# A fixed order on every engine, and q and k turned a block at a time, in chunked attention with routed experts

## The chip, the cores and the metric

The kernel runs on one core of a Trainium2 chip. The metric is device microseconds of one launch, from the start of the program to its end. The core has five instruction queues: TensorE (PE; its weight loads are shown apart as PEld), VectorE (DVE), ScalarE (ACT), GpSimd (POOL) and SyncE (SP), which here only issues DMAs. Each queue runs its instructions strictly in the order in which they stand; semaphores make one wait for another.

## The reference

All data is float32. Attention runs on 4 batches x 8 heads x 768 positions x 64, in chunks of 32 queries that see 8 memory keys, the chunk, 16 keys to its left and 8 to its right. Its output, as 3072 tokens x 512, goes to the best of 8 experts each:

```python
for c in range(nc):                                   # nc = 24 chunks
    k_full = np.concatenate([mem_k, k_ctx], axis=2)
    v_full = np.concatenate([mem_v, v_ctx], axis=2)
    scores = scale * np.matmul(q_c, k_full.transpose(0, 1, 3, 2))
    a = np.exp(scores - np.max(scores, axis=-1, keepdims=True))
    a = a / (np.sum(a, axis=-1, keepdims=True) + 1e-09)
    out[:, :, c_start:c_end] = np.matmul(a, v_full)
...
logits = x @ w_gate
expert_idx = np.argmax(logits, axis=1)
...
h = np.maximum(x_sorted[lo:hi] @ w1[e], 0.0)          # per expert e
y_sorted[lo:hi] = h @ w2[e]
return gate_w[:, None] * y
```

## The kernel before, in words

There are two stages. The first is attention in 32 blocks of 96 queries (QB = 96; 8 blocks make a batch), all 8 heads of a block together. The second is the experts: 31 slots of 128 tokens, each with the w1 and w2 (2 MB each) of its expert. The change touches the first stage alone.

A block i goes through these functions, whose tile names are the names in the rows below. `load_v` brings the 128 keys' values of the block (tile v; three DMAs on SP: keys, 8 memory rows, keys). `scores` multiplies the turned keys kT with the turned queries qT into sc (4 matmuls in the code, which the trace shows as 8) and takes three exponentials on ACT into ex. `values` multiplies ex with v into o, heads 0 to 3 and then heads 4 to 7 (16 matmuls in the trace), and DVE divides by the sums (a RECIPROCAL, then a TENSOR_TENSOR into x); POOL then sends x to DRAM. `turn_xb` turns x by four transposes into tx, which DVE or ACT copies to xT. `logits` multiplies xT with the gate matrix into lg_ps (8 matmuls in the trace), which DVE copies to lg. After the eighth block of a batch `route` ranks its tokens: some twenty small DVE instructions, one on ACT, eight additions in a row on POOL (seen), and two small matmuls (rk).

The queries and keys are loaded and turned by halves of a batch, 384 positions at a time (`load_half`: three DMAs of 128 rows for q and three for k; `turn_half`, called three times for a half: four transposes of k into tk, two DVE copies, four transposes of q into tq, two ACT copies to strided columns). The memory keys are turned once (`turn_mem`), and POOL copies them between the keys of each batch. A half serves four blocks; its three turns stand at three of the steps before.

Nothing in the code fixes the order of the queues: the functions are called in a plain loop, and the tile scheduler, which has its own costs and priorities, sets the order on each queue. So the turns of q and k come two or three times in a row, scores run ahead of values, and the work of neighbouring blocks is mixed.

Of the kernel before, what the change touches and what calls it, by code (L numbers as in the profile page):

```python
# [64 lines left out]
HALF = S // 2  # L65
NT = HALF // 128
# [3 lines left out]
NV = 6  # L70


def window(qb):
    return min(max(PER * qb - LEFT, 0), KW - WIN)
# [10 lines left out]
def runs_of(qb):  # L85

    out = []
    for p in range(WIN):
        kind, x = column(window(qb) + p)
        if out and out[-1][1] == kind and out[-1][2] + out[-1][3] == x:  # L90
            out[-1][3] += 1
        else:
            out.append([p, kind, x, 1])
    return out
# [394 lines left out]
def ordinary(ctx, tc, q, k, v, mem_k, mem_v, moe_w_gate, moe_w1, moe_w2, out, good):  # L489
# [16 lines left out]
    lpool = actx.enter_context(tc.tile_pool(name="lpool", bufs=2))  # L506
# [24 lines left out]
    mk = kpool.tile([B * NMEM, H, D], F32, name="mk")  # L531
    for b in range(B):
        nc.scalar.dma_start(mk[NMEM * b : NMEM * b + NMEM], mem_k[b].rearrange("h m d -> m h d"))


    qTs = [kpool.tile([128, H // 2, 2, HALF], F32, name=f"qT{i}") for i in range(2)]
# [19 lines left out]
    half = [dict() for _ in range(2 * B)]  # L556
    turned = {}

    def load_half(m):
        b, hf = divmod(m, 2)  # L560
        for name, src in (("q", q), ("k", k)):
            t = half[m][name] = lpool.tile([128, NT, H, D], F32, name=f"{name}n")
            by = src[b, :, HALF * hf : HALF * hf + HALF].rearrange("h (p t) d -> p t h d", t=NT)
            for j in range(NT):
                nc.sync.dma_start(t[:, j], by[:, j])

    def load_v(i):
        b, qb = divmod(i, NQB)
        st[i]["v"] = vs[i % NV]
        for p, kind, r, n in runs_of(qb):  # L570
            src = (mem_v if kind == "mem" else v)[b, :, r : r + n].rearrange("h r d -> r h d")
            nc.sync.dma_start(st[i]["v"][p : p + n, :, 0:D], src)

    def turn_mem():
        tm = ps_t.tile([128, H // 2, B * NMEM], F32, tag="t", name="tm")
        for a in range(H // 2):
            turn(tm[:, a], mk[:, 2 * a : 2 * a + 2].rearrange("p h d -> p (h d)"), ident[0 : B * NMEM, 0 : B * NMEM])
        turned["mem"] = kpool.tile([128, H // 2, B * NMEM], F32, name="mkT")
        nc.scalar.copy(turned["mem"], tm)

    def turn_half(m, j):

        b, hf = divmod(m, 2)
        if hf == 0 and j == 0:
            turned["k", b] = apool.tile([128, H // 2, KW], F32, name="kT")
            nc.gpsimd.tensor_copy(
                turned["k", b].rearrange("p a (n c) -> p a n c", c=PER)[:, :, :, QB // 2 : QB // 2 + NMEM],
                bc(turned["mem"][:, :, NMEM * b : NMEM * b + NMEM], 2, NQB),
            )
        kT = turned["k", b].rearrange("p a (n c) -> p a n c", c=PER)  # L590
        qT = turned["q", m] = qTs[m % 2]
        tk = ps_t.tile([128, H // 2, 128], F32, tag="t", name="tk")
        for a in range(H // 2):
            turn(tk[:, a], half[m]["k"][:, j, 2 * a : 2 * a + 2].rearrange("p h d -> p (h d)"), ident)  # L594
        by = tk.rearrange("p a (n f c) -> p a n f c", n=NQB // 2, f=2)
        for f in range(2):
            c0 = (QB // 2 + NMEM) * f + j
            nc.vector.tensor_copy(  # L598
                kT[:, :, hf * NQB // 2 : (hf + 1) * NQB // 2, c0 : c0 + QB // 2 - NT + 1 : NT], by[:, :, :, f]
            )  # L600
        tq = ps_t.tile([128, H // 2, 128], F32, tag="t", name="tq")
        for a in range(H // 2):
            turn(tq[:, a], half[m]["q"][:, j, 2 * a : 2 * a + 2].rearrange("p h d -> p (h d)"), ident)  # L603
        for x in range(2):
            sl = slice(D * x, D * x + D)
            nc.scalar.copy(qT[sl, :, x, j : j + HALF - NT + 1 : NT], tq[sl])  # L606

    def scores(i):
        s, (b, qb) = st[i], divmod(i, NQB)
        kT, qT = turned["k", b], turned["q", i // (NQB // 2)]  # L610
        q0 = QB * (qb % (NQB // 2))
        w0 = window(qb)
        sc = ps_s.tile([128, 2, 512], F32, tag="s", name="sc")
        for a in range(H // 2):
            o = sc[:, a // 2, 2 * QB * (a % 2) : 2 * QB * (a % 2) + 2 * QB]
            mm(  # L616
                o.rearrange("p (x t) -> p x t", x=2),
                lhsT=kT[:, a, w0 : w0 + WIN],
                rhs=qT[:, a, :, q0 : q0 + QB],
                start=True,  # L620
                stop=True,
            )
        ex = s["ex"] = apool.tile([128, H, QB], F32, name="ex", bufs=3)
        x = 0 if qb == 0 else 2 if qb == NQB - 1 else 1
        sc4 = sc[:, :, 0 : 4 * QB].rearrange("p g (h t) -> p g h t", h=4)
        ex4 = ex.rearrange("p (g h) t -> p g h t", g=2)
        for g in range(3):
            sl = slice(CHUNK * g, CHUNK * g + CHUNK)
            nc.scalar.activation(  # L629
                ex4[:, :, :, sl], sc4[:, :, :, sl], AF.Exp, bias=mask[:, 3 * x + g : 3 * x + g + 1], scale=D**-0.5  # L630
            )

    def values(i):
        s = st[i]
        s["x"] = apool.tile([QB, H, D], F32, name="x", bufs=3)
        for g in range(2):
            o = ps_o.tile([QB, 4, D + 1], F32, tag="o", name="o")
            for j in range(4):
                h = 4 * g + j
                mm(o[:, j], lhsT=s["ex"][:, h], rhs=s["v"][:, h], start=True, stop=True)  # L640

            inv = inv_all[:, i, 4 * g : 4 * g + 4]
            nc.vector.reciprocal(inv, o[:, :, D])
            nc.vector.tensor_tensor(s["x"][:, 4 * g : 4 * g + 4], o[:, :, 0:D], bc(inv, 2, D), op=OP.mult)  # L644
        s["x"] = s["x"].rearrange("p h d -> p (h d)")
        nc.gpsimd.dma_start(x_dram[QB * i : QB * i + QB], s["x"])  # L646

    def turn_xb(i):
        s = st[i]
        tx = ps_t.tile([128, DM // 128, QB], F32, tag="t", name="tx")  # L650
        for c in range(DM // 128):
            turn(tx[:, c], s["x"][:, 128 * c : 128 * c + 128], ident[0:QB, 0:QB])  # L652
        s["xT"] = apool.tile([128, DM // 128, QB], F32, name="xT")
        (nc.vector.tensor_copy, nc.scalar.copy)[i % 2](s["xT"], tx)
# [3 lines left out]
    def logits(i):  # L658
        s, (b, t) = st[i], divmod(i, NQB)
        if t == 0:  # L660
            lgs[b] = rpool.tile([QB, NQB, E], F32, name="lg")
        ps = ps_t.tile([QB, E], F32, tag="t", name="lg_ps")
        for c in range(DM // 128):
            mm(ps, lhsT=s["xT"][:, c], rhs=wg[:, c], start=c == 0, stop=c == DM // 128 - 1)  # L664
        nc.vector.tensor_copy(lgs[b][:, t], ps)
        if t == NQB - 1:
            route(b)


    def small(shape, name, dt=F32):  # L670
        return rpool.tile(shape, dt, name=name)

    def route(b):
# [12 lines left out]
        nc.vector.tensor_tensor(oh, bc(rev[0:QB], 1, NQB), bc(first, 2, E), op=OP.is_equal)  # L686

        nc.vector.tensor_tensor(l, l, bc(top, 2, E), op=OP.subtract)
        nc.scalar.activation(l, l, AF.Exp)
        total = small([QB, NQB], "total")  # L690
        nc.vector.reduce_sum(total, l, axis=AX_X)
        nc.vector.tensor_scalar(total, total, 1e-9, None, op0=OP.add)
        nc.vector.reciprocal(gate[:, sl], total)

# [4 lines left out]
        mm(rk, lhsT=ones[0:QB, 0:QB], rhs=seen[:, sl], start=False, stop=True)  # L699
        own = small([QB, NQB, E], "own")  # L700
        nc.vector.tensor_tensor(own, rk, oh, op=OP.mult)
        rank = small([QB, NQB], "rank")
        nc.vector.reduce_sum(rank, own, axis=AX_X)
        ri = small([QB, 3, NQB], "ri", I32)
# [5 lines left out]
        nc.vector.tensor_copy(low, ri[:, 1])  # L710
        for t in range(NQB):
            nc.vector.tensor_scalar(
                row_of[:, t0 + t], iota[0:QB], low[:, t : t + 1], None, op0=OP.is_equal
            )


    load_half(0)
    load_v(0)
    load_v(1)
    load_half(1)  # L720
    turn_mem()
    for j in range(NT):
        turn_half(0, j)
    for i in range(NB + 3):
        m = i // (NQB // 2)
        if i % (NQB // 2) == 1 and m + 2 < 2 * B:
            load_half(m + 2)
        if i + 2 < NB:
            load_v(i + 2)
        if i < NB:  # L730
            scores(i)
        if i % (NQB // 2) < NT and m + 1 < 2 * B:
            turn_half(m + 1, i % (NQB // 2))
        if 0 <= i - 3 < NB:
            logits(i - 3)
        if 0 <= i - 1 < NB:
            values(i - 1)
        if 0 <= i - 2 < NB:
            turn_xb(i - 2)
# [174 lines left out]
```

## Time and profile before

| | |
|---|---|
| three runs | 720.2, 721.64 and 726.11 us; median 721.64 |
| the profiled execution | 721.35 us; its span from first to last instruction 719.6 us |
| the page's share of busy time | PE 90%, PEld 71%, DVE 19%, ACT 18%, POOL 13% |
| mean granted clock of TensorE | 0.927 of 2.4 GHz |
| bytes moved by DMA | 172.78 MB, 240 GB/s over the span |

The profile is of one execution. The span is what lies between the first and the last instruction, so 1.75 us of the time lie outside it. The share of PE is a mean over two stages with different limits, and a matmul that runs at the lower of the two clocks (1.2 in place of 2.4 GHz) counts as busy for about twice as long, so the share alone does not tell how much of the time could be had back. Matmuls overlap, so the distance from the start of one group to the start of the next, where nothing waits, is what a group costs; the length in a row is longer by the tail of its last matmul.

### The profile page before, as it was taken

To read this page: it belongs to the slowest core of one execution; us is meant where nothing else is said; L and a number is where in the kernel's file an instruction comes from. 1 tells how busy PE (TensorE), PEld (TensorE's weight loads), DVE (VectorE), ACT (ScalarE), POOL (GpSimd) and SP (SyncE) were. 2 spreads that over 40 slices of the span, in tenths; PEclk is the share of its full clock that TensorE was granted. 3 is DMA by queue.
4 is the path that set the end of the run, shared out by engine and by line. 5 is a ranking of instruction groups with operands and counts; after the bars stand their busy time and mean duration, and the time that the engine had idled before them with its cause. 6 is when DMAs were issued, how large, how long until landed. Compare 5 with 4: busy or idle time off the path is not lost. (4 is left out here: it accounts for less than half of the span.)

```text
span 719.6 us, 9964 instructions
## 1 busy us (share of the span) xinstructions
PE 648.2 (90%) x4036; PEld 510.3 (71%) x4036; DVE 137.6 (19%) x406; ACT 127.0 (18%) x228; POOL 92.1 (13%) x144
## 2 busy tenths in 40 slices
PE   2888898898883699999999999999999999999991
PEld 2887787788772677776777677767776777677760
DVE  3334534435425010010001000100010001000100
ACT  3554435345200001100110011001100110011000
POOL 2001101101102111111111111111111111111000
PEclk9999969969955579999999999999999999999996
DMA  9999837723212948998899989998899889998800
GB/s 182 206 171 179 173 68 153 166 53 77 73 34 92 392 155 302 321 337 325 313 322 334 342 302 319 333 338 323 314 336 328 325 308 332 328 328 297 319 3 3
DMA packets 140520, 172.78 MB, mean 240 GB/s; under 512 B 87662, under 2 KB 87790, under 8 KB 140464
## 3 DMA queue, kind: packets, MB, share of 16 engines
q1 hardware_dynamic: 132496, 151.01, 66.9%
q0 software_dynamic: 7008, 20.72, 8.4%
q8 instruction: 34, 0.56, 0.3%
q10 hardware_dynamic: 960, 0.32, 0.2%
q14 instruction: 22, 0.18, 0.1%
HBM read 159.44 MB, written 14.42 MB: 242 GB/s over the span
## 5 line engine op out<-in xcount | busy, mean ns | idle before, releaser
L835 PEld LDWEIGHTS ph<-xsT,w 128*128 128x128 f32 x1984 | 228.4, 193 | 14.6 <-issue 14.4
L835 PE MATMUL ph<-xsT,w 128*128 128x128 f32 x1984 | 228.7, 277 | 0.0
L852 PE MATMUL py<-w,h 128*128 128x512 f32 x496 | 218.0, 592 | 0.0
L852 PEld LDWEIGHTS py<-w,h 128*128 128x128 f32 x496 | 91.9, 190 | 103.7 <-issue 103.7
L844 DVE TENSOR_SCALAR h<-ph 128x512 f32<-128x512 f32 x31 | 21.5, 692 | 403.7 <-issue 381.7
L854 ACT ACTIVATE y<-py,gates 128x512 f32<-128x512 f32 x31 | 21.3, 687 | 317.9 <-PE py L852 308.1
L616 PE MATMUL sc<-qT,kT 128*128 128x192 f32 x256 | 58.3, 354 | 9.2 <-ACT ex L629 4.2
L855 POOL DMA_INDIRECT out_dram<-y,dst x31 | 31.5, 1016 | 242.5 <-ACT y L854 242.5
L640 PE MATMUL o<-v,ex 128*96 128x65 f32 x512 | 58.5, 276 | 1.4 <-ACT ex L629 1.4
L640 PEld LDWEIGHTS o<-v,ex 128*96 128x96 f32 x512 | 57.0, 193 | 1.9 <-ACT ex L629 1.9
L812 POOL DMA_INDIRECT xs<-x_dram,src x31 | 30.2, 974 | 170.0 <-PE txs L823 154.6
L616 PEld LDWEIGHTS sc<-qT,kT 128*128 128x128 f32 x256 | 42.3, 199 | 13.0 <-ACT ex L629 6.1
L629 ACT ACTIVATE ex<-sc,cst 128x256 f32<-128x256 f32 x96 | 38.5, 471 | 70.8 <-PE o L640 63.2
L606 ACT COPY qT<-tq 64x512 f32<-64x512 f32 x48 | 40.0, 834 | 31.8 <-PE tq L603 29.8
L846 ACT ACTIVATE h<-ph 128x512 f32<-128x512 f32 x31 | 18.5, 597 | 126.6 <-PE ph L835 126.6
L664 PEld LDWEIGHTS lg_ps<-wg,xT 128*96 128x96 f32 x256 | 29.7, 192 | 13.5 <-PE tq L603 7.3
L664 PE MATMUL lg_ps<-wg,xT 128*96 128x8 f32 x256 | 30.5, 246 | 8.8 <-DVE kT L598 5.2
L646 POOL DMA_DIRECT2D x_dram<-x x32 | 16.6, 520 | 163.6 <-DVE x L644 159.0
L652 PE MATMUL tx<-cst,x 96*128 96x96 f32 x128 | 24.2, 287 | 4.9 <-DVE x L644 2.8
L644 DVE TENSOR_TENSOR x<-o,inv_all 96x256 f32<-96x256 f32 x64 | 26.9, 420 | 2.1
L823 PE MATMUL txs<-cst,xs 128*128 128x128 f32 x124 | 19.4, 283 | 6.9 <-DMA xs<-x_dram,src 6.9
L598 DVE COPY kT<-tk 128x256 f32<-128x256 f32 x48 | 20.5, 487 | 26.6 <-PE tk L594 23.9
(76 smaller groups left out, 225.9 us busy)
## 6 DMA issues: line engine op xcount, KB each, us to landing
w<-in_moe_w_dram SPq DMA_DIRECT2D x62, 2048.0 KB
qn<-in_q_dram SPq DMA_DIRECT2D x24, 256.0 KB
kn<-in_k_dram SPq DMA_DIRECT2D x24, 256.0 KB
x_dram<-x POOLq DMA_DIRECT2D x32, 192.0 KB, 3.0
v<-in_v_dram SPq DMA_DIRECT2D x24, 128.0 KB
v<-in_v_dram SPq DMA_DIRECT2D x24, 112.0 KB
v<-in_v_dram SPq DMA_DIRECT2D x8, 144.0 KB
v<-in_v_dram SPq DMA_DIRECT2D x8, 96.0 KB
```

The lines of the kernel that those rows point to most:

```text
L606: nc.scalar.copy(qT[sl, :, x, j : j + HALF - NT + 1 : NT], tq[sl])
L616: mm(o.rearrange("p (x t) -> p x t", x=2), lhsT=kT[:, a, w0 : w0 + WIN], rhs=qT[:, a, :, q0 : q0 + QB], start=True, stop=True,)
L629: nc.scalar.activation(ex4[:, :, :, sl], sc4[:, :, :, sl], AF.Exp, bias=mask[:, 3 * x + g : 3 * x + g + 1], scale=D**-0.5)
L640: mm(o[:, j], lhsT=s["ex"][:, h], rhs=s["v"][:, h], start=True, stop=True)
L644: nc.vector.tensor_tensor(s["x"][:, 4 * g : 4 * g + 4], o[:, :, 0:D], bc(inv, 2, D), op=OP.mult)
L652: turn(tx[:, c], s["x"][:, 128 * c : 128 * c + 128], ident[0:QB, 0:QB])
L664: mm(ps, lhsT=s["xT"][:, c], rhs=wg[:, c], start=c == 0, stop=c == DM // 128 - 1)
L812: nc.gpsimd.indirect_dma_start(out=s["x"], out_offset=None, in_=x_dram, in_offset=bass.IndirectOffsetOnAxis(ap=src[:, a : a + 1], axis=0),)
L835: mm(ph[:, f], lhsT=s["w1"][:, c, c0 : c0 + 128], rhs=s["xT"][:, c], start=c == 0, stop=c == DM // 128 - 1,)
L844: nc.vector.tensor_scalar(o, ph, 0.0, None, op0=OP.max)
L852: mm(py, lhsT=s["h"][:, f], rhs=s["w2"][:, f], start=f == 0, stop=f == F // 128 - 1)
L855: nc.gpsimd.indirect_dma_start(out=out, out_offset=bass.IndirectOffsetOnAxis(ap=dst[:, a : a + 1], axis=0), in_=y, in_offset=None, bounds_ ...
```

## The change

The first stage is written inside `tc.manual_schedule()`: every queue now runs its instructions in the order in which the code calls them. q and k are loaded and turned a block at a time: `load_q` is one DMA of 96 rows, `load_k` brings the block's 96 keys with the 8 memory keys already between them (three DMAs of 48, 8 and 48 rows), and `turn_q` and `turn_k` are four transposes each, with two ACT copies and one DVE copy. `load_half`, `turn_mem` and POOL's copies of the memory keys go. The loads have four buffers in place of two and are called two to four blocks ahead, ex has two buffers in place of three, and there are four qT tiles of a block in place of two of a half. `values` is called by halves with `turn_xb` of the block before between them. The logits are written to the unused end of the PSUM bank that holds the second half of o; ACT alone copies xT. `route` becomes a generator that the loop advances by one piece in each step.

```diff
+    def load_k(i):
+        st[i]["kn"] = lpool.tile([PER, H, D], F32, name="kn")
+        load_runs(st[i]["kn"], i, PER * (i % NQB), PER, k, mem_k)
...
+    def turn_k(i):
         b, qb = divmod(i, NQB)
...
+            turn(tk[:, a], st[i]["kn"][:, 2 * a : 2 * a + 2].rearrange("p h d -> p (h d)"), ident[0:PER, 0:PER])
+        nc.vector.tensor_copy(turned[b][:, :, PER * qb : PER * qb + PER], tk)
...
+        bank = ps_o.tile([QB, 512], F32, tag="o", name="o")
+        o = bank[:, 0 : 4 * (D + 1)].rearrange("p (h d) -> p h d", h=4)
...
+        return bank[:, 4 * (D + 1) :]
...
-        ps = ps_t.tile([QB, E], F32, tag="t", name="lg_ps")
+        ps = room[:, 0:E]
...
         for t in range(t0, t0 + NQB):
             nc.gpsimd.tensor_tensor(seen[:, t + 1], seen[:, t], onehot[:, t], op=OP.add)
         rk = ps_t.tile([QB, NQB, E], F32, tag="t", name="rk")
         mm(rk, lhsT=tri[0:QB, 0:QB], rhs=oh, start=True, stop=False)
         mm(rk, lhsT=ones[0:QB, 0:QB], rhs=seen[:, sl], start=False, stop=True)
+        yield 1
...
+    def routing(room=None):
+        if work and next(work[0], None) is None:
+            work.pop(0)
+
+    with tc.manual_schedule():
...
+        for i in range(NB + 3):
+            need(i + 4, load_k)
+            need(i + 3, load_q)
+            need(i + 2, load_v)
+            need(i + 2, turn_q)
+            need(i, scores)
+            if 0 <= i - 1 < NB:
+                values(i - 1, 0)
+            need(i - 2, turn_xb)
+            if 0 <= i - 1 < NB:
+                room = values(i - 1, 1)
+            else:
+                room = ps_o.tile([QB, 512], F32, tag="o", name="o")
+            need(i + 3, turn_k)
+            if 0 <= i - 3 < NB:
+                logits(i - 3, room)
+                if (i - 3) % NQB == NQB - 1:
+                    work.append(route((i - 3) // NQB))
+            routing()
+        while work:
+            routing()
```

**On PE in a step of the loop.** Before, around the end of a batch, this stands in a row (tk and tq are the turns of k and q, lg_ps the logits, sc the scores, o the values, tx the turns of x):

```order
L616 MATMUL sc<-qT_101,kT 128x192 x4
L640 MATMUL o<-v_110,ex 96x65 x8
L616 MATMUL sc<-qT_101,kT 128x192 x4
L594 MATMUL tk<-cst,kn 128x128 x4
L603 MATMUL tq<-cst,qn 128x128 x4
L664 MATMUL lg_ps<-wg,xT 96x8 x4
L652 MATMUL tx<-cst,x 128x96 x4
L594 MATMUL tk<-cst,kn 128x128 x4
L603 MATMUL tq<-cst,qn 128x128 x4
L664 MATMUL lg_ps<-wg,xT 96x8 x4
L640 MATMUL o<-v_111,ex 96x65 x8
```

Two sets of turns and logits stand between one scores and the next values. Now every step reads like this one, of block 12 (its scores read qT_95), with the values of block 11 (v_112):

```order
L574 MATMUL tq<-cst,qn 128x96 x4
L593 MATMUL sc<-qT_95,kT 128x192 x4
L619 MATMUL o<-v_112,ex 96x65 x4
L633 MATMUL tx<-cst,x 128x96 x4
L619 MATMUL o<-v_112,ex 96x65 x4
L584 MATMUL tk<-cst,kn 128x104 x4
L645 MATMUL o<-wg,xT 96x8 x4
```

Scores and values come once in every step. The logits stand last and write into the bank of the second o; between that o and them stand only the four turns of k.

**On PE and POOL where a batch is ranked.** At the end of the step of block 13 the two rk matmuls stand in PE's queue, ahead of the next step's turns and scores:

```order
L619 MATMUL o<-v_107,ex 96x65 x4
L584 MATMUL tk<-cst,kn 128x104 x4
L645 MATMUL o<-wg,xT 96x8 x4
L680 MATMUL rk<-onehot,cst 96x64
L681 MATMUL rk<-seen,ones 96x64
L574 MATMUL tq<-cst,qn 128x96 x4
```

On POOL the additions that the second rk waits for (seen) stand behind the stores of x of blocks 0 to 12, the last of which waits for the values of the same step:

```order
L541 MEMSET seen 96x8
L626 DMA x_dram<-x 96x512 x13
L678 ISA
L678 TENSOR_TENSOR seen<-seen,onehot 96x8 x8
L626 DMA x_dram<-x 96x512 x9
```

The rk of the next two batches stand in the same way in the steps of blocks 22 and 31 (nine stores further each), and the last one after the loop. Before, the two rk and the additions had other work between them.

**On SP.** Before, the loads of v for a block, then those of a half, then v again:

```order
L572 DMA v_106<-in_v_dram 56x8x64
L565 DMA qn<-in_q_dram 128x8x64 x3
L565 DMA kn<-in_k_dram 128x8x64 x3
L572 DMA v_107<-in_v_dram 64x8x64
L572 DMA v_107<-in_mem_v_dram 8x8x64
L572 DMA v_107<-in_v_dram 56x8x64
```

Now a step of the loop:

```order
L555 DMA kn<-in_k_dram 48x8x64
L555 DMA kn<-in_mem_k_dram 8x8x64
L555 DMA kn<-in_k_dram 48x8x64
L560 DMA qn<-in_q_dram 96x8x64
L555 DMA v_110<-in_v_dram 64x8x64
L555 DMA v_110<-in_mem_v_dram 8x8x64
L555 DMA v_110<-in_v_dram 56x8x64
```

A step issues seven DMAs, where before it issued three, and six larger ones for every four blocks.

## Rows read from the trace of the kernel before

**Rows 1.** Windows by stage: start:end, length, busy of each engine, clock, DMA, GB/s

```profile
0.00:18.70 18.70, 5.34 (x28) 4.08 (x29) 5.41 (x9) 6.53 (x8) 3.96 (x15) 1.00 1.12 183
18.70:219.40 200.70, 175.80 (x1332) 158.89 (x1332) 83.00 (x293) 80.39 (x157) 22.15 (x58) 0.87 0.60 122
219.40:252.90 33.50, 15.76 (x72) 15.39 (x73) 9.09 (x43) 0.26 (x1) 7.27 (x12) 0.50 0.71 266
252.90:719.60 466.70, 451.29 (x2604) 331.95 (x2604) 40.14 (x62) 39.80 (x62) 58.70 (x59) 0.98 0.82 291
```

**Rows 2.** Windows inside the attention stage, same columns

```profile
54.00:92.00 38.00, 32.45 (x273) 29.04 (x272) 18.52 (x68) 15.38 (x31) 5.47 (x16) 0.99 0.86 169
92.00:105.50 13.50, 13.02 (x71) 12.06 (x70) 3.80 (x13) 6.20 (x11) 1.02 (x2) 0.50 0.21 48
...
143.00:157.00 14.00, 13.38 (x73) 12.59 (x73) 4.58 (x15) 6.21 (x11) 1.02 (x2) 0.51 0.18 41
...
197.70:219.40 21.70, 17.61 (x97) 15.19 (x96) 6.99 (x23) 2.16 (x5) 2.05 (x4) 0.50 0.13 37
```

**Rows 3.** Timeline of PE at the full clock: start, length, operation, count

```profile
28.83 0.60 PE L594 MATMUL tk<-cst,kn 128*128 128x128 f32 x4
...
29.70 1.16 PE L640 MATMUL o<-v,ex 128*96 128x65 f32 x12
30.69 0.50 PE L652 MATMUL tx<-cst,x 96*128 96x96 f32 x4
31.03 1.49 PE L616 MATMUL sc<-qT,kT 128*128 128x192 f32 x8
32.36 0.77 PE L664 MATMUL lg_ps<-wg,xT 128*96 128x8 f32 x8
32.98 1.55 PE L640 MATMUL o<-v,ex 128*96 128x65 f32 x16
```

**Rows 4.** Timeline of PE where the clock falls

```profile
89.25 0.81 PE L664 MATMUL lg_ps<-wg,xT 128*96 128x8 f32 x8 [0.66 <-DVE kT L598]
...
91.52 0.78 PE L603 MATMUL tq<-cst,qn 128*128 128x128 f32 x4 [0.21 <-DVE xT L654]
...
93.64 2.80 PE L640 MATMUL o<-v,ex 128*96 128x65 f32 x16
```

**Rows 5.** Timeline of all engines, last blocks and the ranking after them

```profile
187.33 1.50 PE L640 MATMUL o<-v,ex 128*96 128x65 f32 x16
...
189.07 0.42 DVE L644 TENSOR_TENSOR x<-o,inv_all 96x256 f32<-96x256 f32 x1
189.55 0.20 PEld L652 LDWEIGHTS tx<-cst,x 96*128 96x128 f32 x2 [0.42 <-DVE x L644]
...
189.79 0.51 POOL L646 DMA_DIRECT2D x_dram<-x  x1 [4.45 <-DVE x L644]
...
219.28 0.16 DVE L665 COPY lg<-lg_ps 96x8 f32<-96x8 f32 x1 [1.64 <-PE lg_ps L664]
...
220.87 2.12 POOL L696 TENSOR_TENSOR seen<-seen,onehot 96x8 f32<-96x8 f32 x8 [3.53 <-DVE total L691]
...
224.69 1.65 DVE L712 TENSOR_SCALAR row_of<-cst,low 96x128 f32<-96x128 f32 x8
```

**Rows 6.** Timeline of all engines, the start; SPq rows are DMA issues

```profile
3.26 4.26 SPq L565 DMA_DIRECT2D kn<-in_k_dram  x3
...
10.09 1.11 PE L594 MATMUL tk<-cst,kn 128*128 128x128 f32 x4
...
14.34 0.60 PE L594 MATMUL tk<-cst,kn 128*128 128x128 f32 x4
...
24.33 3.89 SPq L565 DMA_DIRECT2D kn<-in_k_dram  x3
...
33.25 0.54 SPq L572 DMA_DIRECT2D v<-in_mem_v_dram  x1
...
34.93 0.52 SPq L572 DMA_DIRECT2D v<-in_mem_v_dram  x1
```

More of the change, by code (lines that the diff above doesn't have):

```diff
@@ L61, in _consts_general @@
     return np.ascontiguousarray(pack), at
-HALF = S // 2
-NT = HALF // 128
 WIN = 128
@@ L69 @@
 KW = NQB * PER
-NV = 6
+NV, NQ = 6, 4
 def window(qb):
@@ L82, in column, with runs @@
     return "key", QB * blk + (r if r < QB // 2 else r - NMEM)
-def runs_of(qb):
+def runs(start, n):
     out = []
-    for p in range(WIN):
-        kind, x = column(window(qb) + p)
+    for p in range(n):
+        kind, x = column(start + p)
         if out and out[-1][1] == kind and out[-1][2] + out[-1][3] == x:
@@ L505, in ordinary @@
     kpool = actx.enter_context(tc.tile_pool(name="kpool", bufs=1))
-    lpool = actx.enter_context(tc.tile_pool(name="lpool", bufs=2))
+    lpool = actx.enter_context(tc.tile_pool(name="lpool", bufs=4))
     apool = actx.enter_context(tc.tile_pool(name="apool", bufs=2))
@@ L529, in ordinary @@
     nc.scalar.dma_start(wg, moe_w_gate.rearrange("(c p) e -> p c e", p=128))
[L531 to L536, printed above, removed]
+    qTs = [kpool.tile([128, H // 2, 2, QB], F32, name=f"qT{i}") for i in range(NQ)]
     for i, t in enumerate(qTs):
@@ L555, in ordinary @@
     st = [dict() for _ in range(NB)]
-    half = [dict() for _ in range(2 * B)]
     turned = {}
[L559 to L565, printed above, removed]
-    def load_v(i):
-        b, qb = divmod(i, NQB)
[L569 to L572, printed above, removed]
@@ L574, in turn_mem @@
-    def turn_mem():
-        tm = ps_t.tile([128, H // 2, B * NMEM], F32, tag="t", name="tm")
-        for a in range(H // 2):
[L577 to L606, printed above, removed]
@@ new lines, in load_runs, with load_q @@
+    def load_runs(to, i, start, n, src, mem):
+        for p, kind, r, n in runs(start, n):
+            ap = (mem if kind == "mem" else src)[i // NQB, :, r : r + n].rearrange("h r d -> r h d")
+            nc.sync.dma_start(to[p : p + n], ap)
+    def load_q(i):
+        b, qb = divmod(i, NQB)
+        t = st[i]["qn"] = lpool.tile([QB, H, D], F32, name="qn")
+        nc.sync.dma_start(t, q[b, :, QB * qb : QB * qb + QB].rearrange("h r d -> r h d"))
+    def load_k(i):
+        st[i]["kn"] = lpool.tile([PER, H, D], F32, name="kn")
+        load_runs(st[i]["kn"], i, PER * (i % NQB), PER, k, mem_k)
@@ new lines, in load_v, with turn_q @@
+    def load_v(i):
+        st[i]["v"] = vs[i % NV]
+        load_runs(st[i]["v"][:, :, 0:D], i, window(i % NQB), WIN, v, mem_v)
+    def turn_q(i):
+        qT = st[i]["qT"] = qTs[i % NQ]
+        tq = ps_t.tile([128, H // 2, QB], F32, tag="t", name="tq")
+        for a in range(H // 2):
+            turn(tq[:, a], st[i]["qn"][:, 2 * a : 2 * a + 2].rearrange("p h d -> p (h d)"), ident[0:QB, 0:QB])
+        for x in range(2):
+            nc.scalar.copy(qT[D * x : D * x + D, :, x], tq[D * x : D * x + D])
@@ L608, in scores @@
+    def turn_k(i):
+        b, qb = divmod(i, NQB)
+        if qb == 0:
+            turned[b] = apool.tile([128, H // 2, KW], F32, name="kT")
+        tk = ps_t.tile([128, H // 2, PER], F32, tag="t", name="tk")
+        for a in range(H // 2):
+            turn(tk[:, a], st[i]["kn"][:, 2 * a : 2 * a + 2].rearrange("p h d -> p (h d)"), ident[0:PER, 0:PER])
+        nc.vector.tensor_copy(turned[b][:, :, PER * qb : PER * qb + PER], tk)
     def scores(i):
         s, (b, qb) = st[i], divmod(i, NQB)
-        kT, qT = turned["k", b], turned["q", i // (NQB // 2)]
@@ L611, in scores @@
-        q0 = QB * (qb % (NQB // 2))
         w0 = window(qb)
@@ L617, in scores @@
                 o.rearrange("p (x t) -> p x t", x=2),
-                lhsT=kT[:, a, w0 : w0 + WIN],
-                rhs=qT[:, a, :, q0 : q0 + QB],
+                lhsT=turned[b][:, a, w0 : w0 + WIN],
+                rhs=s["qT"][:, a],
                 start=True,
@@ L622, in scores @@
             )
-        ex = s["ex"] = apool.tile([128, H, QB], F32, name="ex", bufs=3)
+        ex = s["ex"] = apool.tile([128, H, QB], F32, name="ex")
         x = 0 if qb == 0 else 2 if qb == NQB - 1 else 1
@@ L631, in scores, with values @@
             )
-    def values(i):
+    def values(i, g):
         s = st[i]
[L635 to L646, printed above, removed]
+        if g == 0:
+            s["x"] = apool.tile([QB, H, D], F32, name="x", bufs=3)
+        bank = ps_o.tile([QB, 512], F32, tag="o", name="o")
+        o = bank[:, 0 : 4 * (D + 1)].rearrange("p (h d) -> p h d", h=4)
+        for j in range(4):
+            h = 4 * g + j
+            mm(o[:, j], lhsT=s["ex"][:, h], rhs=s["v"][:, h], start=True, stop=True)
+        inv = inv_all[:, i, 4 * g : 4 * g + 4]
+        nc.vector.reciprocal(inv, o[:, :, D])
+        nc.vector.tensor_tensor(s["x"][:, 4 * g : 4 * g + 4], o[:, :, 0:D], bc(inv, 2, D), op=OP.mult)
+        if g == 1:
+            s["x"] = s["x"].rearrange("p h d -> p (h d)")
+            nc.gpsimd.dma_start(x_dram[QB * i : QB * i + QB], s["x"])
+        return bank[:, 4 * (D + 1) :]
     def turn_xb(i):
@@ L653, in turn_xb, with logits @@
         s["xT"] = apool.tile([128, DM // 128, QB], F32, name="xT")
-        (nc.vector.tensor_copy, nc.scalar.copy)[i % 2](s["xT"], tx)
+        nc.scalar.copy(s["xT"], tx)
     lgs = {}
-    def logits(i):
+    def logits(i, room):
         s, (b, t) = st[i], divmod(i, NQB)
@@ L665, in logits @@
         nc.vector.tensor_copy(lgs[b][:, t], ps)
-        if t == NQB - 1:
-            route(b)
     def small(shape, name, dt=F32):
@@ L686, in route @@
         nc.vector.tensor_tensor(oh, bc(rev[0:QB], 1, NQB), bc(first, 2, E), op=OP.is_equal)
+        yield 1
         nc.vector.tensor_tensor(l, l, bc(top, 2, E), op=OP.subtract)
         nc.scalar.activation(l, l, AF.Exp)
+        yield 1
         total = small([QB, NQB], "total")
@@ L693, in route @@
         nc.vector.reciprocal(gate[:, sl], total)
+        yield 1
         for t in range(t0, t0 + NQB):
@@ L699, in route @@
         mm(rk, lhsT=ones[0:QB, 0:QB], rhs=seen[:, sl], start=False, stop=True)
+        yield 1
         own = small([QB, NQB, E], "own")
@@ L703, in route @@
         nc.vector.reduce_sum(rank, own, axis=AX_X)
+        yield 1
         ri = small([QB, 3, NQB], "ri", I32)
@@ L710, in route @@
         nc.vector.tensor_copy(low, ri[:, 1])
+        yield 1
         for t in range(NQB):
@@ L714, in route, with need @@
             )
[L717 to L739, printed above, removed]
+            if t % 3 == 2:
+                yield 1
+    def need(i, f, *lists):
+        if 0 <= i < NB:
+            f(i)
+    work = []
+    def routing(room=None):
+        if work and next(work[0], None) is None:
+            work.pop(0)
+    with tc.manual_schedule():
+        for i in range(3):
+            load_k(i)
+            load_q(i)
+            if i < 2:
+                load_v(i)
+        load_k(3)
+        turn_k(0)
+        turn_q(0)
+        turn_k(1)
+        turn_q(1)
+        turn_k(2)
+        for i in range(NB + 3):
[19 more added lines that the diff above has]
+            routing()
     ok = cpool.tile([QB, 2, NB, H], F32, name="ok")
```

## The prediction

> **What bounds the kernel now.** I read the stages first. Up to 18.7 us the core waits for its first loads, from there to 219.4 us it runs the attention blocks, from there to 252.9 us it ranks the tokens and loads the first experts, and the rest, 466.7 us, is expert work with PE busy in 451 of it [rows 1]. The change touches the first two stretches. The last two start from the last logits copy at 219.28 us and have the same instructions as before, so I move them as one block.
>
> Inside the 200.7 us of attention, PE is busy for 175.8, yet DVE and ACT for only about 83 and 80 and DMA for 0.60 [rows 1]. So PE's order decides. Windows over that stretch split it in two kinds [rows 2]. At a granted clock of 0.99 PE still idles 5.6 of 38 us. At 0.50 it is busy nearly all the time, and slow: 13.5, 14.0 and 21.7 us, together 49.2. At the full clock the same work would take about half, so some 24 us lie here. Before the first of these falls PE had run logits, turns and little else for about four microseconds, with waits between; afterwards sixteen value matmuls take 2.80 us, which take 1.55 elsewhere [rows 3, 4]. In the third stretch, 197.7 to 219.4, there are no scores left to run, and each block's chain of values, division, turn and logits stands bare.
>
> **What a block needs.** From start to start where nothing waits [rows 3]: eight turns of 128 columns take 29.70 - 28.83 = 0.87 us, 0.109 each; twelve value matmuls 0.99, so sixteen 1.32; four turns of x 0.34; eight scores 1.33; eight logits 0.62. Before, a block has on average six turns of q and k (24 for four blocks), 0.65 us: 4.26 in all, 136 us for 32 blocks. Of 200.7 us, then, 136 is work at the full clock, some 24 the low clock and some 40 idle time.
>
> **The change, part by part.** The new turns are eight a block, but narrower: four of 96 columns at the price of x's turns, 0.34, and four of 104, 0.36. A block's work becomes 4.31 us, 0.05 more. ACT's copies of q become contiguous, DVE's copy of k one in place of parts, POOL's copies of the memory keys go; all of this lies beside PE, since DVE and ACT have about 2.6 and 2.5 us of work a block now [rows 1].
>
> The order adds a wait in each step. The logits write the bank that DVE is still reading for the second half of x. In the trace the end of a values group to the first turn that needs its x is 187.33 + 1.50 to 189.55, 0.72 us; PE could have started 0.17 earlier than that end, as a turn does at 30.69 against 29.70 + 1.16 [rows 3, 5]. That makes 0.89, of which the four turns of k fill 0.36: 0.53 us left. Behind the logits on PE stand the next turns of q and all scores, so the wait is on the path. The step becomes 4.84 us. Each step also has new waits for DMA on PE (k, q, v); the trace shows none for such steps. They cost nothing if already satisfied, and at most about what PE idles today, 5.6 us in 38, that is 0.9 a block of 6.2, less the 0.53 already counted: 0 to 0.4. I take 0.15, nearer the low end, because PE's idle rows name engines and not such checks. **Step: 5.0 us.**
>
> SP must feed this. Three loads of 1,024 short rows take 3.89 us to issue, 1.30 each, and a block's v (three DMAs, as many rows) 34.93 - 33.25 = 1.68 [rows 6]. A step now wants 0.81 of such a load for k with one small DMA more (0.5), 0.75 for q, and v: 1.05 + 0.5 + 0.98 + 1.68 = 4.2 us. That is under 5.0, and the buffers let SP run some three blocks ahead, so PE hides it; if that cover went, the step would be what DMA gives.
>
> Start: ahead of the first scores stand k, q and two v of blocks 0 to 2, 1.71 MB, and 0.25 MB of constants. At the 183 GB/s of the first stretch that is 10.7 us after the first bytes [rows 1]; in the trace the first k is issued at 3.26 and turned at 10.09 [rows 6], so a load is several microseconds on its way. I take the first scores at 14 us, bounds 12 and 18.7 (as now). The next three steps have little PE work and go as loads come, 4 us each: block 3 starts at 26. From there 28 steps of 5.0 bring the scores of block 31 to 166.
>
> Ranking: in the steps of blocks 13, 22 and 31 PE meets the second rk matmul while POOL still has to store the same step's x (0.51) and do eight additions (2.12) [rows 5]. These start when DVE's division ends, as the logits do. So PE waits 2.63 - 0.62 - 0.1 = 1.9 us. Two of these lie ahead of the last scores, 3.8 us. They also leave PE with turns, logits and idle time for some 4 us, like the stretch in rows 4. I expect the clock to fall in each, and to come back with the next scores: half of a 7 us stretch, 3.4 us each, bounds 0 and 6.7 (half of the 13.5 of rows 2). Scores of block 31 then start at 166 + 3.8 + 6.8 = 176.6.
>
> Tail: block 31's step without new turns and with the third rk, 4.31 - 0.70 + 0.53 + 1.9 = 6.0; the next 0.34 + 1.32 + 0.62 + 0.53 = 2.8; turn, copy and logits of the last block 2.2. That is 11.0 us at the full clock. Scores are gone here as they were after 197.7, so I add 5 for the low clock (bounds 0 and 9). The last logits copy ends at about 192.6. One batch's ranking is still unfinished there, and its eight row_of instructions, 1.65 us [rows 5], now stand ahead of the last ranking: 194.3. Before, that copy ended at 219.44.
>
> **Sum:** 194.3 - 219.44 = -25.1 us. Against the profiled execution's 721.35 that is 696.2; the median of the three runs, 721.64, is the same within 0.3, so **I forecast 696 us**.
>
> **A rule against it.** Between 10.09 and 14.34 us PE ran only turns, and four of them went from 1.11 to 0.60 us: turning alone brought the clock from 1.2 to 2.4 GHz [rows 6]. The Trainium skill says otherwise (TensorE: Matmul & The Clock Gate, Part 4): transposes do not count as work that raises the clock. By that rule the 1.0 us of turns in each new step would be as good as idle time, and the third rival below would be the likely one. The trace disagrees with it here.
>
> **The rivals.** First, *no falls*: the clock holds through the rk waits and the tail and the step is 4.84. That takes off 6.8 + 5 + 28 x 0.16 = 16 us: 680. For it: from 54 to 92 us the clock held through many half-microsecond waits. Against it: no row shows it holding through 4 us without scores.
>
> Second, *the loads bound the step*. In the busiest loading DMA's share was already 0.86 with only 6.2 us a block [rows 2], a step of 5.0 wants as many bytes, and seven DMAs share the queue. If SP and DMA give 5.6 us a step, the time is 696 + 28 x 0.6 = 713. It would show as PE waiting for DMA ahead of turns. Against it stands the sum of 4.2.
>
> Third, on the slow side, *the clock does not hold in the ordinary step*. Each step now has 3.5 us from the end of its scores to the next scores, with values as the only large work between. If that lets the clock fall, work of 4.31 doubles while the wait of 0.53 vanishes: 3.8 us more per such step. The forecast's 25 us are gone after 25 / 3.8 = 6.6 such steps beyond the two counted; with ten, the time is 734. For it: before the fall of rows 4 PE was not idle, only poor in scores and values. Against it: there neither scores nor values ran at all, here 2.65 of 5 us are theirs, more than the 2.65 of 6.3 that held from 54 to 92.
>
> That the order is not what the code says is no rival; the built order shows it.
>
> **How the numbers follow.** The forecast's case gets 0.66, no falls 0.13, loads 0.12, the clock 0.05, and 0.04 is left for what I have not thought of. The forecast's own bounds: with steps of 4.9, one fall less and a short tail about 686; with steps of 5.2 and full falls about 708. The range takes in the first rival and the second to its larger side: 678 to 715. About 1%, 7 us, is what a measurement of this kernel can tell from no change. Faster by over 1% (under 714) then holds 0.66 + 0.13 + half of the loads' case and some of the rest, 0.86; same 0.08; slower 0.06.
>
> **What would show it.** Right: PE's row reads the same in every step, 4.8 to 5.2 us from scores to scores; logits wait for DVE some 0.5 us in most steps; rk waits for POOL about 1.9 us three times; low clock only there, at the start and in the tail; the last logits copy near 193, and everything after it as long as before. Wrong: PE waits for loads in the middle of the stage, a low clock in ordinary steps, or a change behind the last logits.

## The result, and the profile after

| | before | this |
|---|---|---|
| median of the device times | 723.76 us (720.2 to 726.11, 4 runs) | 693.11 us (689.9 to 695.51, 4 runs) |
| ratio, 95% interval | | 0.9578 [0.9514, 0.9642] |
| profiled execution | 721.35 us | 695.51 us, span 693.7 |

The change makes the kernel 30.7 us, 4.2%, faster; the forecast was 696 us, 25.1 us less. That forecast was made from the profiled execution, and between the two profiled executions lie 25.8 us. The profiled execution of this kernel is the slowest of its four (granted clock 0.946; the others 0.951 to 0.955), so by the medians the gain is 5.6 us larger than forecast. Of the other executions there is no trace, so where these 5.6 us lie is open. Line numbers of the new kernel differ: scores L593, values L619, division L622 and L623, turns of x L633, of q L574, of k L584, ranking L678 to L697. The logits, L645, appear as "o", since they stand in the bank of the values.

First the windows by stage of the kernel after, then windows inside its attention, with the columns of [rows 1]: start:end, length, busy time (and instructions) of PE, PEld, DVE, ACT, POOL, the granted clock, DMA's share, GB/s.

```profile
0.00:16.00 16.00, 5.09 (x25) 3.86 (x25) 3.45 (x8) 3.17 (x5) 2.02 (x15) 1.00 1.09 152
16.00:192.60 176.60, 156.72 (x1398) 149.95 (x1396) 69.76 (x256) 79.52 (x191) 21.39 (x56) 0.93 0.75 146
192.60:229.70 37.10, 17.68 (x80) 16.82 (x81) 11.64 (x52) 0.26 (x1) 7.80 (x13) 0.50 0.66 248
229.70:693.70 464.00, 448.91 (x2598) 329.95 (x2596) 39.45 (x61) 39.81 (x62) 58.17 (x59) 0.99 0.81 293
...
55.00:75.00 20.00, 18.55 (x181) 17.75 (x181) 8.80 (x31) 10.07 (x24) 2.05 (x4) 1.00 1.08 202
...
86.30:89.70 3.40, 3.23 (x13) 3.23 (x14) 0.00 (x0) 0.94 (x2) 0.32 (x2) 0.50 0.98 166
134.10:140.90 6.80, 6.39 (x32) 6.35 (x33) 0.60 (x2) 2.63 (x6) 0.48 (x3) 0.50 0.41 82
181.80:192.60 10.80, 8.47 (x52) 8.05 (x51) 3.48 (x18) 0.96 (x2) 1.88 (x8) 0.50 0.12 36
```

Against [rows 1] the gain is all in attention: from the first scores to the last logits 176.6 us instead of 200.7, and the start is 2.7 shorter. What follows the last logits copy has hardly changed: 501.1 us of span remain after it starts, 500.3 before. Against [rows 2] the low clock inside attention is down from 49.2 us to 21 (3.4, 6.8 and 10.8), and a fourth stretch of some 3 us lies in the start, from 24.97.

PE's timeline of the kernel after, as in [rows 3, 4]: start in us, length, operation, and in brackets the idle time before it and what ended it. The first rows are the start, then comes one ordinary step, then the step of block 13 with the first ranking.

```profile
5.33 0.93 PE L584 MATMUL tk<-cst,kn 104*128 104x104 f32 x4 [5.33 <-DMA kn<-in_k_dram]
...
15.95 2.51 PE L593 MATMUL sc<-qT,kT 128*128 128x192 f32 x8
...
24.97 0.87 PE L574 MATMUL tq<-cst,qn 96*128 96x96 f32 x4 [1.71 <-DMA qn<-in_q_dram]
...
30.59 1.49 PE L593 MATMUL sc<-qT,kT 128*128 128x192 f32 x8
...
55.21 1.49 PE L593 MATMUL sc<-qT,kT 128*128 128x192 f32 x8
56.54 0.81 PE L619 MATMUL o<-v,ex 128*96 128x65 f32 x8
57.19 0.50 PE L633 MATMUL tx<-cst,x 96*128 96x96 f32 x4
57.53 0.82 PE L619 MATMUL o<-v,ex 128*96 128x65 f32 x8
58.18 0.53 PE L584 MATMUL tk<-cst,kn 104*128 104x104 f32 x4
59.07 0.84 PE L645 MATMUL o<-wg,xT 128*96 128x8 f32 x8 [0.36 <-DVE x L623]
59.77 0.53 PE L574 MATMUL tq<-cst,qn 96*128 96x96 f32 x4
60.14 1.49 PE L593 MATMUL sc<-qT,kT 128*128 128x192 f32 x8
...
83.71 0.84 PE L645 MATMUL o<-wg,xT 128*96 128x8 f32 x8 [0.37 <-DVE x L623]
84.41 0.36 PE L680 MATMUL rk<-onehot,cst 96*96 96x64 f32 x2
86.47 0.58 PE L681 MATMUL rk<-seen,ones 96*96 96x64 f32 x2 [1.71 <-POOL seen L678]
86.85 0.85 PE L574 MATMUL tq<-cst,qn 96*128 96x96 f32 x4
87.49 2.58 PE L593 MATMUL sc<-qT,kT 128*128 128x192 f32 x8
```

From 55.21 to 60.14 is one step, 4.93 us, and nearly all read alike: the hand-made order with its one idle time, ahead of the logits. In the last rows the second rk matmul waits 1.71 us for POOL's additions, and the eight scores after it take 2.58 us where they took 1.49: the clock has fallen. The chain of events in the end part, timeline of all engines, answers to [rows 5]:

```profile
181.58 2.13 POOL L678 TENSOR_TENSOR seen<-seen,onehot 96x8 f32<-96x8 f32 x8
...
192.58 0.16 DVE L646 COPY lg<-o 96x8 f32<-96x8 f32 x1 [0.49 <-PE o L645]
192.66 1.65 DVE L697 TENSOR_SCALAR row_of<-cst,low 96x128 f32<-96x128 f32 x8
```

The eight row_of instructions end at 194.31. And the waits of the same kernel up to 230 us, summed by what was waited for (total, times, longest):

```profile
PEld o L645 <- DVE x L623: 16.1, 28, 0.9
...
PE tk L584 <- DMA kn<-in_k_dram: 10.3, 3, 5.3
...
PE rk L681 <- POOL seen L678: 5.9, 4, 1.7
...
PE tq L574 <- DMA qn<-in_q_dram: 2.3, 2, 1.7
```

PE waits for the loads in the start only: the three waits of tk end at 5.33, 9.33 and 14.37, and the two of tq at 10.83 and 24.97. In the steps two things remain, the logits' wait for the division and rk's for POOL.

### The profile page after: what moved, and what is told of

It is laid out like the page before. It is cut to its first block, busy times and chain, and to the rows that moved or that the text cites. A ratio compares the mean times of both kernels' runs of the same rounds, so it can differ in the third digit from the quotient of the medians.

```text
span 693.7 us, 10193 instructions
## 1 busy us (share of the span) xinstructions
PE 628.4 (91%) x4096; PEld 500.6 (72%) x4096; DVE 124.3 (18%) x376; ACT 122.8 (18%) x259; POOL 89.4 (13%) x142
## 5 line engine op out<-in xcount | busy, mean ns | idle before, releaser
L619 PE MATMUL o<-v,ex 128*96 128x65 f32 x512 | 54.4, 251 | 0.0
L619 PEld LDWEIGHTS o<-v,ex 128*96 128x96 f32 x512 | 53.4, 172 | 0.1
L593 PE MATMUL sc<-qT,kT 128*128 128x192 f32 x256 | 52.6, 353 | 0.0
L593 PEld LDWEIGHTS sc<-qT,kT 128*128 128x128 f32 x256 | 45.5, 208 | 0.0
L576 ACT COPY qT<-tq 64x384 f32<-64x384 f32 x64 | 30.2, 472 | 69.1 <-PE tq L574 68.7
L645 PE MATMUL o<-wg,xT 128*96 128x8 f32 x256 | 28.5, 238 | 12.3 <-DVE x L623 12.2
L645 PEld LDWEIGHTS o<-wg,xT 128*96 128x96 f32 x256 | 25.9, 175 | 18.0 <-DVE x L623 16.1
L584 PE MATMUL tk<-cst,kn 104*128 104x104 f32 x128 | 18.1, 267 | 10.4 <-DMA kn<-in_k_dram 10.3
L623 DVE TENSOR_TENSOR x<-o,inv_all 96x256 f32<-96x256 f32 x64 | 26.9, 420 | 2.2
L622 DVE RECIPROCAL inv_all<-o 96x4 f32<-96x4 f32 x64 | 11.4, 179 | 84.1 <-PE o L619 84.0
```

Of the source, the lines that this page charges most:

```text
L576: nc.scalar.copy(qT[D * x : D * x + D, :, x], tq[D * x : D * x + D])
L593: mm(o.rearrange("p (x t) -> p x t", x=2), lhsT=turned[b][:, a, w0 : w0 + WIN], rhs=s["qT"][:, a], start=True, stop=True,)
```

## Experiments

Diffs are against the kernel after where nothing else is said; each ratio is to the kernel before, timed beside it. "Steps" are the distances from scores to scores.

**1. The logits' wait.** The logits' eight columns go into the spare part of the bank of the first half of o, which DVE has read by then.

```
-                values(i - 1, 0)
+                room = values(i - 1, 0)
...
-                room = values(i - 1, 1)
+                values(i - 1, 1)
```

> The logits go to the bank of the first half of o, which DVE has read long before, so their wait for DVE (16.1 us over 28 steps in the changed kernel's trace) is gone. If that wait is on the path as the prediction says, a step falls from 4.93 to about 4.4 us and the time from 693 to about 678. If the loads are the next bound, steps come out at 4.6 to 4.8, PE shows waits for DMA, and the time is 683 to 689. If the wait only hid another wait of the same length, nothing changes.

Measured: 677.67 us (676.71 to 680.44), ratio 0.9361 [0.9301, 0.9421]. Ordinary steps took 4.32 us, the sum of a block's PE work (4.31). PE's timeline of this kernel:

```profile
59.60 0.53 PE L584 MATMUL tk<-cst,kn 104*128 104x104 f32 x4
59.96 0.77 PE L645 MATMUL o<-wg,xT 128*96 128x8 f32 x8
60.59 0.53 PE L574 MATMUL tq<-cst,qn 96*128 96x96 f32 x4
```

The logits now follow the turns of k without idle time. So the choice of a bank cost 0.60 us a step and some 15 us in all, half of what the whole change brought, and the loads carry steps of 4.32 as well. Both rk waits stayed (2.3 and 2.2 us), and their low clock too.

**2. The ranking's wait.** Two pieces of the ranking go into one step and rk gets a step of its own: POOL's additions come a step earlier, rk stays in the step in which it stood.

```
         nc.vector.tensor_tensor(oh, ...)
-        yield 1
...
             nc.gpsimd.tensor_tensor(seen[:, t + 1], ...)
+        yield 1
         rk = ps_t.tile([QB, NQB, E], F32, tag="t", name="rk")
```

> The eight additions on POOL run one step ahead of the matmul that reads them; the number of pieces of the ranking stays the same. If the waits of rk and the two falls of the clock behind them belong together, as the prediction says, the steps of blocks 13, 14, 22 and 23 (7.65, 6.01, 7.55 and 7.51 us) fall to about 4.93 and the third wait goes from the tail: 9 + 1.8, so about 682. If the clock falls there for another reason, only the waits go, 5.5 us, and the falls stay: about 688.

Measured: 684.81 us (680.0 to 685.62), ratio 0.9432 [0.9365, 0.9498]. From the scores of block 3 to those of block 31 it takes 138.0 us instead of 146.3. PE's timeline at the first ranking, at the last logits and scores ahead of the end part, and a window of this kernel:

```profile
83.02 0.36 PE L680 MATMUL rk<-onehot,cst 96*96 96x64 f32 x2
83.22 0.33 PE L681 MATMUL rk<-seen,ones 96*96 96x64 f32 x2
...
161.80 0.84 PE L645 MATMUL o<-wg,xT 128*96 128x8 f32 x8 [0.72 <-DVE x L623]
...
166.51 0.81 PE L645 MATMUL o<-wg,xT 128*96 128x8 f32 x8 [0.82 <-DVE x L623]
167.18 2.56 PE L593 MATMUL sc<-qT,kT 128*128 128x192 f32 x8
...
20.80:167.60 146.80, 135.04 (x1294) 129.03 (x1293) 64.53 (x233) 74.60 (x180) 19.18 (x48) 1.00 0.84 168
```

The clock stays at its upper level for 146.8 us. The waits in after's two rankings ahead of block 31 come to 3.4 us, yet 8.3 went: the clock that fell behind them cost more than they did. The third wait, in the end part, gave 0.7 us and not the 1.8 expected (15.1 us from the scores of block 31 to the last logits copy, 15.8 in after).

**3. The scheduler's order instead of the hand-made one**, with all else of the change.

```
-    with tc.manual_schedule():
+    with ExitStack():
```

> The changed kernel with the tile scheduler's order in place of the order of the code; loads, turns, buffers and the ranking's pieces as changed. If the fixed order brings the gain, the time goes back to 710 to 725, with falls of the clock and bare tails as before. If loading and turning a block at a time brings it, the time stays at 690 to 700.

**4. The hand-made order without the rest.** The kernel before, its loop in the order in which it is written (diff against before):

```
+    with tc.manual_schedule():
         load_half(0)
         load_v(0)
         ...
         for i in range(NB + 3):
             ...
```

> The kernel before with its calls in a fixed order: halves, buffers and the ranking in one lump as before. If the fixed order brings the gain alone, steps near 4.8 us, a lump of about 4 us with a fall of the clock once a batch, and the old start give about 710, with 700 to 716 as bounds. If the old loads and turns stand in the way of any order, it comes out at 720 or above.

Measured: 3, 710.73 us (709.55 to 715.32), 0.9829 [0.9761, 0.9896]; 4, 701.24 us (698.13 to 703.05), 0.9673 [0.9609, 0.9738], nine under the 710 expected but inside its bounds. One row each, 3 from its waits, 4 from PE's timeline:

```profile
PE tk L584 <- ACT qT L576: 19.4, 27, 0.7
```

```profile
68.24 0.82 PE L664 MATMUL lg_ps<-wg,xT 128*96 128x8 f32 x8 [0.61 <-DVE kT L598]
70.57 0.38 PE L698 MATMUL rk<-onehot,cst 96*96 96x64 f32 x2 [1.52 <-DVE onehot L686]
72.58 0.58 PE L699 MATMUL rk<-seen,ones 96*96 96x64 f32 x2 [1.62 <-POOL seen L696]
72.95 2.77 PE L640 MATMUL o<-v,ex 128*96 128x65 f32 x16
```

In 3 the turns of k come behind ACT's copy of q, 0.7 us in nearly every step (5.54), and the clock falls six times ahead of the end part. In 4 the fixed order alone brings most of the gain. Its steps are 5.37 us with turns and 3.68 in the one of four without, 4.95 on average: about the 4.93 of the kernel after, although q and k still come in halves. It has a wait of its own: in the steps with turns the logits wait some 0.6 us for DVE's copy of k. What it loses lies at the rankings, which there stand in one piece: about 23 us more than ordinary steps in three of them (10.9 + 4.7 where 5.37 + 3.68 is ordinary, and so on), with two waits of about 1.5 us and the fallen clock in each.

**5. The spreading of the ranking.** The kernel after with the ranking of a batch emitted at once.

```
-            routing()
-        while work:
-            routing()
+            while work:
+                routing()
```

> The changed kernel with the whole ranking of a batch in one piece behind its last logits. If spreading it has a price and a gain as the terms say, PE waits for DVE's chain and POOL's additions, some 4 us in place of 1.9, three times, and DVE's twenty instructions delay the next division: 2 to 4 us more a batch, less the 1.65 us that no longer stand ahead of the last ranking: 697 to 703. If spreading is worth nothing, the time is 691 to 694.

Measured: 697.65 us (697.15 to 698.86), 0.9636 [0.9578, 0.9694]. PE's timeline at the first ranking of this kernel:

```profile
70.30 0.35 PE L680 MATMUL rk<-onehot,cst 96*96 96x64 f32 x2 [1.61 <-DVE lg L668]
72.20 0.58 PE L681 MATMUL rk<-seen,ones 96*96 96x64 f32 x2 [1.55 <-POOL seen L678]
```

The two waits of 4 are back, and a ranking costs about 6 us (the first has steps of 9.23 + 7.18 for 4.92 each), where after pays 3.8 and 5.2 and has one of the three in the end part. Experiment 5 is the whole change but for the spreading, and is 0.4% faster than 4, with intervals that overlap nearly whole. So the change's 4.2% are: the order 3.3%, the spread ranking some 0.6% (the intervals overlap here too, the ranges of the times do not), and all the rest together 0.4% that is not told from nothing. That rest is the blockwise loading and turning with its buffers, the values by halves and the new place of the logits, and the place of the logits alone costs some 15 us, 2.2% (1); what the blockwise loading is worth without it is not told by 4 against 5. Under the scheduler the spread ranking and the rest bring 1.7% (3). The parts do not simply add.

**6. Both waits gone**: 1 and 2 together.

> The logits in the first half's bank and the additions a step ahead, together. If the two waits are separate terms on the path, as the prediction adds them, the gains add: 693.1 - 15.4 - 8.3 = about 669, with 28 steps of 4.32 us and no fall of the clock before the tail. If the loads take over as the bound once both waits are gone, PE waits for DMA in the middle of the stage and the time is 673 to 680.

Measured: 664.54 us (662.71 to 665.34), 0.9175 [0.9118, 0.9232]. That is 28.6 us less than the kernel after, where 1 and 2 alone give 15.4 and 8.3, and 5 under the 669 expected of their sum. A window of this kernel:

```profile
20.00:162.00 142.00, 138.36 (x1384) 136.98 (x1384) 67.32 (x255) 78.07 (x189) 21.43 (x56) 1.00 0.96 179
```

These 5 us are the end part: from the scores of block 31 to the end of the last logits copy 9.1 us, where 1 needs 14.9, 2 needs 15.1 and after 15.8. The clock falls here only at 162.7, behind the last logits.

**7 and 8. Can the clock be held through the ranking at the end?** On top of 6, unread work is added on PE: 8 matmuls of a score's size, as the trace counts them (two for a call), ahead of the last logits, 32 ahead of the last rk and 48 behind it (in 8, turns of 128 columns that take as long: 12, 48, 72); the count of tokens per expert moves in front of the last of them. Behind the ranking at the end stand who, 64 matmuls that find the token of every place in the slots.

```
+            if i == NB + 1:
+                warm(4)
...
+        warm(16)
         while work:
             routing()
+        warm(24)
```

> The kernel with both changes, and matmuls of the scores' shape whose results nobody reads, put where PE waits in the tail: 8 in the trace ahead of the last logits, 32 ahead of the last rk, 48 behind the count (which moves ahead of them). If the low clock of the tail and of the who matmuls is a price, as the prediction has it, the clock stays at 2.4 GHz to the end of who: who takes 7 in place of 13.5 us and the tail loses 2 to 4, so about 10 less than the kernel with both, 659. If that clock falls whatever PE runs there, the added work costs 0 to 4 us: 669 to 673.

> The same with turns (transposes of 128 columns) in place of the unread matmuls, for about the same time: 12, 48 and 72 of them. If turns count as work that holds the clock, as the start of the kernel before shows by its rows, the result is that with matmuls, about 659. If they do not, which the Trainium skill (TensorE: Matmul & The Clock Gate, Part 4) says, the clock falls as without them: 669 to 675.

Measured: with matmuls 660.58 us (658.57 to 662.95), 0.9133 [0.9075, 0.9192]; with turns 661.25 (659.88 to 662.87), 0.9138 [0.908, 0.9195]. PE's timeline, of the one with matmuls, then of the one with turns and a window of it, and then that of after:

```profile
167.79 8.05 PE L731 MATMUL wm<-ex 128*128 128x192 f32 x48
...
176.93 7.38 PE L811 MATMUL who<-ent,row_of 96*128 96x93 f32 x64 [0.97 <-POOL ent L807]
```

```profile
168.26 8.06 PE L734 MATMUL wm<-cst,ex 128*128 128x128 f32 x72
...
177.40 7.38 PE L814 MATMUL who<-ent,row_of 96*128 96x93 f32 x64 [0.96 <-POOL ent L810]
...
20.70:188.00 167.30, 160.25 (x1589) 158.90 (x1587) 78.92 (x306) 77.89 (x189) 27.93 (x68) 1.00 0.88 185
```

```profile
207.00 13.96 PE L798 MATMUL who<-ent,row_of 96*128 96x93 f32 x64 [8.59 <-POOL ent L794]
```

The 64 who matmuls take 7.38 us instead of 13.96, as expected. The gain over 6 is 4.0 and 3.3 us instead of 10. Of that, the 2 to 4 us expected of the last blocks had already come with 6. In the profiled executions of 6 and 7, who is 6.6 us shorter, the added work puts its start 1.0 us later after the scores of block 31, and what follows who takes 0.8 longer; the medians lie a little closer still. The expected equality of matmuls and turns holds.

**9. The loads.** Each block's v is loaded a second time, into a tile that nobody reads.

```
+        again = lpool.tile([WIN, H, D], F32, name="again", bufs=2)
+        load_runs(again, i, window(i % NQB), WIN, v, mem_v)
```

> The changed kernel, with each block's v loaded a second time into a tile that nobody reads: ten DMAs a step and 1,024 short rows more. By the prediction's price (4.2 us a step for what the change loads, 1.68 more for a second v) the loads now ask for 5.9 us and bound the step: 28 x 0.95 more, about 720, with PE waiting for k and q. If the loads were much cheaper than that sum (3.2 us or less), the step stays at 4.93 and the time at 693 to 696. If they were dearer, the step is over 6.2 and the time over 728.

Measured: 709.61 us (707.84 to 710.41), 0.979 [0.9714, 0.9865], between the first two times expected. A window and a wait of this kernel, and the first and last of ten DMA issues in a row, from SP's timeline (kn at 73.68 begins the next ten):

```profile
40.00:100.00 60.00, 53.01 (x473) 50.60 (x473) 21.92 (x74) 26.56 (x64) 7.22 (x19) 0.93 1.03 203
...
PE tq L576 <- DMA qn<-in_q_dram: 9.2, 9, 2.4
...
68.69 0.39 SPq L555 DMA_DIRECT2D kn<-in_k_dram  x1
...
73.68 0.38 SPq L555 DMA_DIRECT2D kn<-in_k_dram  x1
```

Most steps are still 4.92 us, and some wait for q, up to 2.4 us, with clock falls behind them. Ten DMAs go out in 5.0 us, hardly more than a step. In after, seven go out in 3.6 us at the quickest (from 66.72 to 70.31; the sets before and behind take 4.1 and 4.6). DMA moves 203 GB/s here against 202 in after (the window 55:75 above), so in both the rate is the same and only the bytes differ. A step here moves 1.13 MB (456 rows of 2,048 bytes loaded, 96 stored): at 203 GB/s, 5.57 us by estimate. From the scores of block 3 to those of block 31 the steps average 5.56, rankings included. With DMA's share at 1.03, it is the bytes that set this pace, more than the issuing on SP. In after a step moves 0.87 MB, 4.3 us at 202 GB/s: cover of some 0.6 us at its 4.93, and next to none at the 4.32 of experiments 1 and 6.

**10. First scores earlier.** On top of the kernel with matmuls of 7, v of block 0 is loaded behind k and q of blocks 0 to 2, and v of block 1 behind the fourth k.

```
-            if i < 2:
-                load_v(i)
+        load_v(0)
         load_k(3)
+        load_v(1)
```

> The kernel with both changes and unread matmuls, with the first two v loaded behind k and q of blocks 0 to 2. The first scores come 2 to 2.5 us earlier. If the first three steps go as the loads come, as the prediction says, block 3 starts when it did (30.4 us) and the time stays at 660; if the start is a chain of PE's own, the 2 us last to the end: 658.

Measured: 658.97 us (657.54 to 662.86), 0.9102 [0.9025, 0.9178]. The first scores start at 12.12 instead of 16.33, but those of block 3 at 29.28 instead of 30.40: the second block's scores wait 3.62 us for q. The gain of 1.6 us is inside the spread. That fits a start that is set by all the bytes of the first blocks more than by their order, but does not show it.

## Why the prediction was right

**What bounds the kernel** held: PE's order. Experiment 4 shows it alone (3.3% of 4.2).

**The step** was forecast at 5.0 us and is 4.93. Dense work 4.31 is confirmed by experiment 1 (4.32). The wait behind DVE costs 0.60, forecast 0.53. The 0.15 for waits on loads is nothing: PE waits for loads in the start only. The two errors offset each other to 0.07 a step; from block 3 to block 31, the rankings apart, the steps take 137.3 us instead of 140.

**SP's supply** was priced at 4.2 us a step and takes 3.6 at the quickest. It was hidden either way, as forecast, but the price was too high: in experiment 9 ten DMAs went out in 5.0 us, not 5.9, and the steps averaged 5.56, by their bytes.

**The start** was mis-sized: first scores at 14, measured 15.96, and block 3 at 26, measured 30.59. The 10.7 us for 1.96 MB at 183 GB/s were too few: DMA moved 152 GB/s in the first 16 us (and the k, q and two v are 856 rows of 2,048 bytes, 1.75 MB, not 1.71). The next three steps took 4.9 us on average, not 4, one of them with a fallen clock. That is 4.6 us, the largest error of the sum.

**Ranking**: forecast twice 1.9 us of waiting and 3.4 of clock, 10.6. The waits are 1.7 each; in all the steps of blocks 13 and 14, and 22 and 23, took 3.8 and 5.2 more than ordinary, 9.0. That the clock falls with the wait, and not with the ranking's own work, is what experiment 2 shows.

These errors (+4.6, -2.7, -1.6) leave +0.3: the scores of block 31 start at 176.91, forecast 176.6. **The tail**, 16 us with the low clock, is 15.8. The row_of instructions end at 194.31, forecast 194.3; of the 1.65 us that they were to add ahead of the last ranking, 0.8 show (501.1 against 500.3). So the closeness of the total to the profiled execution rests partly on errors that cancel, and on which execution was profiled; the mechanisms were those named, and 1, 2 and 4 show the logits' wait, rk's wait with its low clock, and the order each by itself.

**The rivals.** The clock did not hold through the rk waits, so not the first; where both waits are gone (6), it held, as the first has it. Steps did not wait for loads, so not the second; it needs more load, as in 9. The third, the slow side, did not come: the clock stood at 1.00 in ordinary steps.

**Whose gain is it?** The prediction did not divide the gain among the parts of the change. The order alone has most of it (4). The blockwise loading, most of the code, came together with a place of the logits that costs some 15 us, so the 0.4% between 4 and 5 is not its own worth: with the better bank the kernel, its ranking spread too, reaches 677.67 (1), where 4 stands at 701.24. Whether halves would do as well with both waits mended was not tried. What the blockwise loading does show is a step that is the same every time.

## What to carry to other kernels

In a fixed order, look at the one idle time that every step repeats, and at what shares a bank with it: one line (experiment 1) was worth half as much as the whole change. Price a wait of two microseconds on TensorE at more than its length where the clock falls behind it, and take it away by a step's distance between maker and user; that wait and the one of every step, taken away together, gave more than their sum (6). Undo the parts one by one before crediting the largest of them.

## What the runs showed of the hardware

- **A busy TensorE alone did not bring the clock back.** In the window after the last logits (192.6 to 229.7) the granted clock is 0.50, although PE runs the 64 who matmuls there without a pause for 13.96 us. With large matmuls (7) or turns (8) ahead of them they took 7.38 us, at the upper level throughout. What in them keeps the clock down was not tried.
- **Turns keep the clock up as matmuls do.** In 8 the granted clock stayed at its upper level, 2.4 GHz, from 20.7 to 188.0 us, with 120 turns in two groups where 7 has 80 matmuls; who took 7.38 us in both. The Trainium skill (TensorE: Matmul & The Clock Gate, Part 4) says that transposes do not count as work for the clock. These turns, in float32, contradict it. The four in [rows 6] do so by their lengths alone: the granted clock is recorded there as 1.00 from 0 to 18.7 us [rows 1], while they take 1.11 and then 0.60 us.
- **The clock also fell without a long wait.** In 2, with no rk wait, it fell at 167.6, behind two steps whose logits waited 0.72 and 0.82 us. In 6, where PE did the same work without these waits, it held up to 162.7, past the last logits.
